# A spectral filter and a token mixer on one core: the first batch's turn, rearranged

## The chip, the core and the metric

The kernel runs on one core of a Trainium2 chip. TensorE (PE) multiplies, VectorE (DVE), ScalarE (ACT) and GpSimd (POOL) work beside it, SyncE (SP) and POOL issue the transfers. The metric is device time in microseconds of one execution; lower is better.

## What is computed

For 8 batches of a 3136 x 256 matrix x: a Fourier filter along the sequence, and on its result u a low-rank mixing of the sequence (rank 32) and an MLP over the channels.

```python
X = np.fft.rfft(x, axis=1)
x = np.fft.irfft(X * (filt_r + 1j * filt_i), n=3136, axis=1)
xt = x.transpose(0, 2, 1)
u = x + (xt @ U @ V).transpose(0, 2, 1)
out = u + np.maximum(u @ w_ch1, 0.0) @ w_ch2      # 256 -> 1024 -> 256
```

## The kernel before

3136 is 64 x 49, and the transform is done in two steps: a 64-point one (F1, constant `w64`) and a 49-point one for each of 32 frequencies s, with the twiddles in it (`t2` forward, `g12` back). Between the two steps the layout changes from sequence rows to frequency rows. For batches 1 to 7 that goes through DRAM: F1 (`f1_units`, 13 units of a batch, each one matmul of 512 columns and a copy to `asb`; after the units 2, 5, 8 and 12 a chunk is stored to `c1`), then `load_a` of eight frequencies at a time, then a *pair* (two frequencies): `forward` to px, the product with the filter on VectorE, and two pairs later the inverse (`i1`) to esb, stored to `c2` every four pairs; `load_e` brings it back as e2. From e2, `h1_unit` makes H1 = U's spectrum times e2, and `make_u` makes u for four rows at a time: a low-rank matmul with V (`vr`) and H1, and four with e2 and the inverse transform `s2`, in one PSUM bank for each half of the channels, copied to `ut`. A *group* of four rows then goes through `mm1` (eight hidden tiles, relu) and `mm2` (with u added through an identity matrix).

Batch 0 has no other batch to hide behind, and goes without DRAM: `first_f1`, `first_a` and `first_mid` transpose on PE instead. `first_mid` runs 16 pairs m; DVE's product of each (128 x 1024) is the densest work there. In the spare time of PE and ACT lie the first units of batch 1 (`next(fill)`), dummy matmuls `keep_on`, and U's spectrum `prep_u` (two PSUM banks, copied by ACT to `usb`). After the last pair, the transposes L389 make e2 in seven pieces (k4), copied by DVE and ACT in turn, and `h1_unit(0)` and `make_u(0)` follow.

V has to come in the order of the rows, on 128 partitions: `v_order` (POOL, L241) reorders it in seven pieces `vp` of 32 partitions, and `v_units` (L248) spreads each with a matmul by `sel` (four identity matrices) and copies it on ACT to `vr`. Piece k serves group k of every batch.

The order of the work is written by hand: each engine does its instructions in the order of the program, and waits follow from data and buffers. The main loop (L670) gives each group eight *slots*; after every two mm1 tiles and after every mm2 row `run(slot)` issues what `put` has placed there: units, pairs (`steps`, L639), loads, V's pieces, H1. Group 0 has no mm2 beside it, so slots 0 to 7 are short. On SP's queue stand the stores of batch 1's chunks, all `load_a`, `load_e` and the stores to `c2`, in the order of the slots; on POOL's the loads of x and, before the main loop, V's reordering between the loads of batch 2's first chunks (L628).

PSUM has eight banks: four "m" (mm1, units, V, u, transposes, batch 0's px), two "o" (mm2, U, batch 0's transposes, early units), one "x" (a pair's px), one "f" (inverse, H1). A bank is written again when its copy is done.

Of the kernel before, what the change touches and what calls it, by code (L numbers as in the profile page):

```python
# [9 lines left out]
F16 = mybir.dt.float16  # L10
# [7 lines left out]
RANK = 32  # L18
ESC = 16.0
NH = 25  # L20
# [5 lines left out]
def _consts():  # L26
    n, half = SEQ, SEQ // 2
    r = np.arange(NR)
    q = np.arange(NQ)


    w = np.zeros((NQ, NS, 2))
    for s in range(NS):
        w[:, s, 0] = np.cos(2 * np.pi * s * q / NQ)
        w[:, s, 1] = -np.sin(2 * np.pi * s * q / NQ)
    w[:, 0, 1] = (-1.0) ** q
    w = w.reshape(NQ, 64)
    w64 = np.zeros((128, 128))
    w64[:64, :64] = w
    w64[64:, 64:] = w  # L40
    s2 = np.zeros((128, 128))
    s2[:64, :64] = w.T / ESC
    s2[64:, 64:] = w.T / ESC


    t2 = np.zeros((NS, 98, 128))
    g = np.zeros((NS, 128, 98))
    for s in range(NS):
        for j in range(49):
            if j < 25:  # L50
                f = s + 64 * j
                e, sg = np.exp(-2j * np.pi * f * r / n), 1.0
            elif s:
                f = 64 * (j - 24) - s
                e, sg = np.exp(-2j * np.pi * (n - f) * r / n), -1.0
            else:
                f = 32 + 64 * (j - 25)
                e, sg = np.exp(-2j * np.pi * f * r / n), 1.0
            ei = np.conj(e)
            if s:  # L60
                t2[s, :49, j], t2[s, 49:, j] = e.real, -e.imag
                t2[s, :49, 64 + j], t2[s, 49:, 64 + j] = sg * e.imag, sg * e.real
                g[s, j] = np.concatenate([ei.real, ei.imag]) * 2
                g[s, 64 + j] = np.concatenate([-ei.imag, ei.real]) * 2 * sg
            else:
                o = 0 if j < 25 else 49
                t2[s, o:o + 49, j] = e.real
                t2[s, o:o + 49, 64 + j] = e.imag
                g[s, j, o:o + 49] = ei.real * (2 if f else 1)
                g[s, 64 + j, o:o + 49] = -ei.imag * 2  # L70

    t2[0, :, 64] = 0
    t2[0, 49:, 64] = (-1.0) ** r
    g[0, 64] = 0
    g[0, 64, 49:] = (-1.0) ** r
    g *= ESC / n
    gs = np.concatenate([g[:, 64:], g[:, :64]], 1)
    f16 = np.float16
    return (w64.astype(f16), s2.astype(f16), np.eye(128).astype(f16),
            np.tile(np.eye(32), (1, 4)).astype(f16),  # L80
            np.ascontiguousarray(t2.transpose(1, 0, 2).reshape(98, NS * 128)).astype(f16),
            np.ascontiguousarray(np.stack([g, gs], 1).transpose(2, 0, 1, 3)
                                 .reshape(128, NS * 2 * 98)).astype(f16))
# [3 lines left out]
def kernel(  # L87
# [30 lines left out]
    def bank(tag, name):  # L118
        return ps.tile([128, 512], F32, tag=tag, bufs=BUFS[tag], name=name)
# [78 lines left out]
    load_rest()  # L198
    for c in range(2, len(CH)):
        load_x(0, c)  # L200
    sel = cst.tile([32, 128], F16)
    nc.sync.dma_start(sel, sel_d.ap())
    s2 = cst.tile([128, 128], F16)
    nc.sync.dma_start(s2, s2_d.ap())
# [24 lines left out]
    usb = cst.tile([128, NH * RANK], F16)  # L229
    nc.vector.memset(usb[64:128, (NH - 1) * RANK:NH * RANK], 0.0)  # L230

    vps = []

    def v_order():

        for r0 in range(0, NH, 4):
            n, nh = (4, 2) if r0 < NH - 1 else (1, 1)
            vp = sb.tile([32, 512], F16, tag="h", bufs=18, name="vp")
            dst = vp[:, 0:n * nh * 64].rearrange("p (r h q) -> p r h q", h=nh, q=64)
            for k, v in enumerate(vqs):  # L240
                nc.gpsimd.tensor_copy(  # L241
                    dst[:, :, :, 32 * k:32 * k + 32],
                    bass.AP(tensor=v.tensor, offset=v.offset + r0,
                            ap=[v.ap[0], [1, n], [NH, nh], [NR, 32]]))
            vps.append((r0, n * nh * 64, vp))
            yield

    def v_units():  # L248

        for r0, n, vp in vps:  # L250
            pv = bank("m", "pv")
            nc.tensor.matmul(pv[:, 0:n], sel[:, :], vp[:, 0:n], start=True, stop=True)
            nc.scalar.copy(vr[:, r0 * 128:r0 * 128 + n], pv[:, 0:n])
            yield

    def new_e2(b):
# [2 lines left out]
        st[b]["e2"] = e2  # L259
        return e2  # L260

    def prep_u():
        for n0, nn in ((0, 16), (16, 9)):
            pu = bank("o", "pu")
            for h in range(2):
                m = (min(nn, NH - h - n0)) * RANK
                a = (h * NH + n0) * RANK
                nc.tensor.matmul(pu[64 * h:64 * h + 64, 0:m], w64[0:64, 0:64], uq[:, a:a + m],
                                 start=True, stop=True)
            m = (min(nn, NH - 1 - n0)) * RANK  # L270
            nc.scalar.copy(usb[:, n0 * RANK:n0 * RANK + m], pu[:, 0:m])
            if m < nn * RANK:
                nc.scalar.copy(usb[0:64, n0 * RANK + m:(n0 + nn) * RANK],
                                      pu[0:64, m:nn * RANK])


    at = sb.tile([128, 2 * 64 * NR], F16, tag="e2", bufs=2, name="at")
# [53 lines left out]
    def first_mid(fill):  # L331
# [26 lines left out]
        for m in range(NS // 2):  # L358
            for k, part in enumerate(PARTS):
                if k and 2 * m == part[0]:  # L360
                    swap_real(*part)
                    swap_imag(*part)
            uv = both_products(m, pxs.pop(0))
            if pend is not None:
                back(*pend)
            pend = (m, uv)
            if m + 2 < NS // 2:
                pxs.append(ahead(m + 2))
            if m + 3 < NS // 2:
                first_a(m + 3)  # L370
            if m in (3, 7, 11):
                keep_on(12)
            if m > 12:
                keep_on(12, "m")
            if m in (9, 10, 11, 14, 15):
                next(fill)
            if m == 14:
                prep_u()
        back(*pend)
        keep_on(8, "m")  # L380
        e2 = new_e2(0)
        for k4, n0 in enumerate(range(0, NH, 4)):
            pt = ps.tile([128, 1024], F16, tag="m", bufs=BUFS["m"], name="pe")
            w = min(4, NH - n0)
            k = 64 if w == 1 else 128
            for rr in range(w):
                for dh in range(2):
                    o, a = rr * DM + dh * 128, (dh * NH + n0 + rr) * 128
                    nc.tensor.transpose(pt[0:k, o:o + 128], et[:, a:a + k], idn[:, :])  # L389
            dst = e2[0:k, n0 * DM:(n0 + w) * DM]  # L390
            (nc.scalar.copy if k4 in (1, 4, 6) else nc.vector.tensor_copy)(dst, pt[0:k, 0:w * DM])
            if k4 == 3:
                next(fill)
            if k4 == 5:
                next(vgen)

    def f1_units(b, both):
        ne = 0
        for c in range(len(CH)):
            xt = st[b]["x"].pop(c)  # L400
            asb = sb.tile([128, 7 * DM], F16, tag="asb", bufs=3, name="asb")
            for n0 in range(0, CH[c], 2):
                w = min(2, CH[c] - n0) * DM
                k = 64 if c0[c] + n0 == NH - 1 else 128
                pf = bank("o" if b == 1 and ne < 6 else "m", "pf")
                nc.tensor.matmul(pf[0:k, 0:w], w64[0:k, 0:k], xt[0:k, n0 * DM:n0 * DM + w],  # L406
                                 start=True, stop=True)
                dst = asb[0:k, n0 * DM:n0 * DM + w]
# [115 lines left out]

    def u_part(b, r0, nr, half, pm, o, dh):

        e2, h1 = st[b]["e2"], st[b]["h1"]
        k = 64 if half else 128
        nc.tensor.matmul(pm[:, o:o + nr * k], h1[:, dh * 128:(dh + 1) * 128],  # L529
                         vr[:, r0 * 128:r0 * 128 + nr * k], start=True, stop=False,  # L530
                         skip_group_check=True)
        for rr in range(nr):
            a = (r0 + rr) * DM + dh * 128
            nc.tensor.matmul(pm[:, o + rr * k:o + (rr + 1) * k], e2[0:k, a:a + 128],  # L534
                             s2[0:k, 0:k], start=False, stop=(rr == nr - 1),
                             skip_group_check=True)

    def make_odd(b):
# [10 lines left out]
    def make_u(gx):  # L549
        b, r0, nr = groups[gx]  # L550
        if nr == 1:
            make_odd(b)
            uts[gx] = odd[b // 2]
            return
        uts[gx] = sb.tile([128, 1024], F16, tag="ut", bufs=3, name="ut")
        for dh in range(2):
            pm = bank("m", "pu")
            u_part(b, r0, nr, False, pm, 0, dh)
            nc.scalar.copy(uts[gx][:, dh * 512:(dh + 1) * 512], pm)  # L559

    def mm1(gx, t):
        w = groups[gx][2] * 128
# [71 lines left out]
    vgen = v_units()  # L634
    first_mid(fill)
    next(h1_unit(0))
    make_u(0)

    steps = [10 + 1.4 * k for k in range(NP)] + [33 + 2.87 * k for k in range(NP)]  # L639
    for k in range(7):  # L640
        put(k // 2, fill)
    for b in range(3, nb):
        steps += [SB * (b - 2) + 31 + 3 * k for k in range(NP)]
    steps += [steps[-1] + 3 * (k + 1) for k in range(LAG)]
# [6 lines left out]
    for b in range(1, nb):  # L651
        for gi in range(NS // KG):
            t = steps[NP * (b - 1) + GP * gi]
            put(t - (5 if b == 1 else 8), one(load_a, b, gi))
        put(SB * b - 4, h1_unit(b))
        if b > 1:
            fill = f1_units(b, b == 2)
# [5 lines left out]
                if b > 2:  # L663
                    put(steps[NP * (b - 1)] - 68 + 10 * c, one(load_x, b, c))

    for k in range((NH - 1) // 4):
        put(1 + 2 * k, vgen)

    slot = 0
    for gx in range(len(groups) + 1):  # L670
# [47 lines left out]
```

## Time and profile before

| | us |
|---|---|
| median of 3 executions | 561.04 |
| lowest, highest | 560.57, 564.15 |
| the profiled execution: time, span | 561.33, 559.6 |
| PE busy in the span | 532.6 (95%) |
| ACT, DVE, POOL busy | 363.3, 367.3, 248.8 |
| PE idle before its px at 66.05, waiting for a load | 1.91 |
| DVE idle before its first e2 copy at 44.69 | 3.19 |
| mean of one pair product of batch 1 on DVE (L448) | 1.219 |
| copies of 128 x 512 from PSUM: ACT L559, DVE L597 | 0.598, 0.692 |

Busy time counts a matmul with its way through the array, so several in a row overlap. The chain of work that ended last is followed back from the end, from each piece to what released it. PEclk is the share of full speed that PE's clock was granted.

### The profile page before, as it was taken

What the parts mean: (1) busy time and instruction counts of PE and PEld (TensorE: products, weight loads), DVE (VectorE), ACT (ScalarE), POOL (GpSimd) and SP (SyncE); (2) the same over time, 40 slices, a digit from 0 to 9 for tenths busy, and PEclk for the clock granted to TensorE, in tenths of its full rate; (3) what the DMA queues carried; (4) which work ended last, traced back from release to release, by engine and by line L of the source; (5) the groups of instructions that cost most, each with busy time, mean ns of one, the idle gap of its engine ahead of it and who ended that gap; (6) DMA issues with size and microseconds to landing.
All of it is one profiled execution on the core that took longest, in us unless ns stands there. A gap on an engine that the chain in (4) does not pass through costs nothing.

```text
span 559.6 us, 11747 instructions
## 1 busy us (share of the span) xinstructions
PE 532.6 (95%) x4530; PEld 381.4 (68%) x4530; DVE 367.3 (66%) x531; ACT 363.3 (65%) x731; POOL 248.8 (44%) x356
## 2 busy tenths in 40 slices
PE   4788899999999999999999999999999999999996
PEld 4675477767677767677776767777677767767665
DVE  7993376657777577767777577767777587424342
ACT  3777666767767586777767586677666576654441
POOL 7678031255556455555556365555444344210000
PEclk9899899999999999999999999999999999999999
DMA  8999669767979857787879757786757544631223
GB/s 139 209 207 227 196 152 224 152 172 172 205 178 212 190 135 164 169 195 184 205 167 204 171 134 166 180 209 166 178 156 156 139 111 96 139 86 42 74 77 84
DMA packets 67897, 89.83 MB, mean 161 GB/s; under 512 B 6881, under 2 KB 53506, under 8 KB 66946
## 3 DMA queue, kind: packets, MB, share of 16 engines
q0 software_dynamic: 19120, 50.37, 40.8%
q1 hardware_dynamic: 48642, 38.65, 28.9%
q8 instruction: 35, 0.57, 0.5%
q14 instruction: 20, 0.16, 0.1%
q10 hardware_dynamic: 80, 0.07, 0.0%
HBM read 56.80 MB, written 48.17 MB: 188 GB/s over the span
## 4 chain that ended last, share of the span: by engine, by line
PE 82%; DVE 4%; DMA 3%; ACT 2%; issue 1%; SPq 0%; ACTq 0%; DVEq 0%
PE po L588 30%; PE phh L566 28%; PE pi L476 4%; PE px L440 4%; PE po L592 4%; PE pu L529 4%; PE pu L534 4%; PE pf L406 3%; DVE uv L461 1%; ACT h L573 1%; DMA e<-c 1%; PE ph L507 1%; DMA c<-esb 1%; DVE uv L459 1%; DMA a<-c 1%
## 5 line engine op out<-in xcount | busy, mean ns | idle before, releaser
L573 ACT ACTIVATE h<-phh 128x512 f16<-128x512 f32 (+1 forms) x350 | 186.6, 575 | 107.0 <-PE phh L566 106.6
L588 PE MATMUL po<-w,h 128*128 128x256 f16 x1568 | 204.0, 273 | 0.0
L566 PE MATMUL phh<-ut,w 128*128 128x512 f16 x768 | 197.7, 379 | 0.6 <-ACT ut L559 0.2
L464 POOL TENSOR_TENSOR y<-uv 128x512 f16<-128x512 f16 x96 | 110.3, 1149 | 150.2 <-DVE uv L461 71.0
L588 PEld LDWEIGHTS <-h 128*128 128x128 f16 x1568 | 150.4, 98 | 36.4
L461 DVE TENSOR_TENSOR uv<-px,ft 64x512 f16<-64x512 f32 x192 | 132.1, 688 | 2.6
L597 DVE COPY och<-po 128x512 f32<-128x512 f32 x96 | 66.4, 692 | 81.8 <-PE po L592 80.4
L566 PEld LDWEIGHTS <-w 128*128 128x128 f16 x832 | 74.7, 98 | 53.1 <-issue 3.5
L459 DVE TENSOR_TENSOR uv<-px,ft 128x512 f16<-128x512 f32 x96 | 66.0, 688 | 56.0 <-PE px L440 54.0
L480 ACT CAST esb<-pi 98x512 f16<-98x512 f32 x112 | 65.8, 588 | 39.7 <-PE pi L476 32.0
L605 POOL DMA_DIRECT2D out_dram<-och x84 | 45.6, 547 | 60.9 <-DVE och L597 60.9
L412 ACT CAST asb<-pf 128x512 f16<-128x512 f32 (+1 forms) x82 | 46.6, 570 | 16.4 <-PE pf L406 16.4
L440 PE MATMUL px<-a,t 98*128 98x256 f16 x256 | 49.6, 276 | 6.6 <-DMA a<-c 2.8
L559 ACT CAST ut<-pu 128x512 f16<-128x512 f32 x96 | 51.8, 598 | 2.2 <-PE pu L534 1.9
L592 PE MATMUL po<-idn,ut 128*128 128x128 f16 x384 | 52.9, 219 | 0.0
L571 DVE TENSOR_SCALAR h<-phh 128x512 f16<-128x512 f32 (+1 forms) x66 | 42.9, 649 | 13.9 <-PE phh L566 13.4
L448 DVE TENSOR_TENSOR uv<-px,ft 128x1024 f16<-128x1024 f32 x32 | 38.0, 1219 | 10.1 <-PE px L440 9.7
L534 PEld LDWEIGHTS <-e 128*128 128x128 f16 (+1 forms) x400 | 30.9, 97 | 17.7 <-issue 2.5
L416 POOL DMA_DIRECT2D c<-asb x48 | 26.0, 548 | 33.9 <-ACT asb L412 26.5
L529 PE MATMUL pu<-vr,h 128*128 128x512 f16 (+1 forms) x112 | 39.6, 354 | 1.4 <-ACT h L511 0.5
L592 PEld LDWEIGHTS <-ut 128*128 128x128 f16 x384 | 37.7, 98 | 4.4
L534 PE MATMUL pu<-s,e 128*128 128x128 f16 (+1 forms) x400 | 40.3, 218 | 0.0
(72 smaller groups left out, 378.5 us busy)
## 6 DMA issues: line engine op xcount, KB each, us to landing
out_dram<-och POOLq DMA_DIRECT2D x84, 256.0 KB, 4.3
a<-c SPq DMA_DIRECT2D x28, 392.0 KB
c<-esb SPq DMA_DIRECT2D x28, 392.0 KB
xt<-in_x_dram POOLq DMA_DIRECT2D x56, 192.0 KB, 5.8
c<-asb POOLq DMA_DIRECT2D x42, 192.0 KB, 3.3
e<-c SPq DMA_DIRECT2D x28, 200.0 KB, 4.4
e<-c SPq DMA_DIRECT2D x28, 192.0 KB, 5.6
out_dram<-och SPq DMA_DIRECT2D x12, 256.0 KB, 3.3
```

The lines of the kernel that those rows point to most:

```text
L440: nc.tensor.matmul(px[:, sl * DM:(sl + 1) * DM], t2[:, s * 128:(s + 1) * 128], a2[:, (2 * ml + sl) * DM:(2 * ml + sl + 1) * DM], start=Tru ...
L459: nc.vector.tensor_mul(uv[:, 0:512], px[:, :], ft[:, a:a + 512])
L461: nc.vector.tensor_mul(uv[p:p + 64, 512:1024], px[q:q + 64, :], ft[q:q + 64, b:b + 512])
L464: nc.gpsimd.tensor_add(y, uv[:, 0:512], uv[:, 512:1024])
L480: nc.scalar.copy(esb[:, ml * 512:(ml + 1) * 512], pi[0:98, :])
L529: nc.tensor.matmul(pm[:, o:o + nr * k], h1[:, dh * 128:(dh + 1) * 128], vr[:, r0 * 128:r0 * 128 + nr * k], start=True, stop=False, skip_gr ...
L534: nc.tensor.matmul(pm[:, o + rr * k:o + (rr + 1) * k], e2[0:k, a:a + 128], s2[0:k, 0:k], start=False, stop=(rr == nr - 1), skip_group_chec ...
L566: nc.tensor.matmul(pm[:, 0:w], w1[:, dh * 1024 + t * 128:dh * 1024 + (t + 1) * 128], ut[:, dh * w:(dh + 1) * w], start=(dh == 0), stop=(dh ...
L573: nc.scalar.activation(h[:, 0:w], pm[:, 0:w], RELU)
L588: nc.tensor.matmul(po[:, o:o + DM], hs[gx, t][:, rr * 128:(rr + 1) * 128], w2[:, t * DM:(t + 1) * DM], start=(t == 0), stop=False, skip_gr ...
L592: nc.tensor.matmul(po[:, o + dh * 128:o + (dh + 1) * 128], ut[:, dh * w + rr * 128:dh * w + (rr + 1) * 128], idn[:, :], start=False, stop= ...
L597: nc.vector.tensor_copy(och[:, a:(rr + 1) * DM], po[:, 0:(rr + 1) * DM - a])
```

## The change

In `first_mid`, batch 1's units come at m = 8, 9, 10, 13, 14, 15 (before: 9, 10, 11, 14, 15 and k4 = 3), the sixth in an "m" bank; the dummy matmuls of m = 15 go. U's matmuls stay at m = 14, both parts in a row; their copies move behind the last pair and from ACT to DVE.

`make_u(0)` becomes `first_u`: the four spectrum matmuls of both halves first, then V's pieces 1 and 2 (before in slots 1 and 3), then the low-rank matmul of each half and its copy, the first on ACT, the second on DVE. V's pieces 0, 1, 2 are copied by DVE, the others by ACT; pieces 3 to 6 come in slots 6, 8, 10, 12 (before 5, 7, 9, 11). Those four have 128 rows: POOL first clears the whole tile (a memset ahead of each reordering), and `sel` has zeros in 96 more rows.

In the main loop, the seven units left come in slots 0, 1, 1, 2, 2, 3, 3 (before 0, 0, 1, 1, 2, 2, 3); batch 1's pairs in slots from 12 on, 1.3 apart (before from 10, 1.4 apart); batch 1's loads six slots before their first pair instead of five, those of the other batches nine instead of eight. The pairs of batch 2 and all that follows keep their slots.

```diff
+    vps = [(r0, 512 if r0 < NH - 1 else 64,
+            sb.tile([128, 512], F16, tag="h", bufs=18, name="vp")) for r0 in range(0, NH, 4)]
     def v_order():
-        for r0 in range(0, NH, 4):
+        for r0, w, vp in vps:
...
-            vp = sb.tile([32, 512], F16, tag="h", bufs=18, name="vp")
-            dst = vp[:, 0:n * nh * 64].rearrange("p (r h q) -> p r h q", h=nh, q=64)
+            if r0 > 8:
+                nc.gpsimd.memset(vp[:, 0:w], 0.0)
+            dst = vp[0:32, 0:n * nh * 64].rearrange("p (r h q) -> p r h q", h=nh, q=64)
...
     def v_units():
...
-            nc.tensor.matmul(pv[:, 0:n], sel[:, :], vp[:, 0:n], start=True, stop=True)
-            nc.scalar.copy(vr[:, r0 * 128:r0 * 128 + n], pv[:, 0:n])
+            k = 128 if r0 > 8 else 32
+            nc.tensor.matmul(pv[:, 0:n], sel[0:k, :], vp[0:k, 0:n], start=True, stop=True)
+            (nc.scalar.copy if r0 > 8 else nc.vector.tensor_copy)(vr[:, r0 * 128:r0 * 128 + n], pv[:, 0:n])
...
-            if m > 12:
+            if m in (13, 14):
                 keep_on(12, "m")
-            if m in (9, 10, 11, 14, 15):
+            if m in (8, 9, 10, 13, 14, 15):
                 next(fill)
             if m == 14:
-                prep_u()
+                pus = [prep_u(0, 16), prep_u(16, 9)]
+                for pu in pus:
+                    next(pu)
         back(*pend)
         keep_on(8, "m")
         e2 = new_e2(0)
+        for pu in pus:
+            next(pu, None)
...
-            if k4 == 3:
-                next(fill)
...
-                pf = bank("o" if b == 1 and ne < 6 else "m", "pf")
+                pf = bank("o" if b == 1 and ne < 5 else "m", "pf")
...
+    def first_u():
+        pms = [bank("m", "pu") for dh in range(2)]
+        for dh in range(2):
+            u_spec(0, 0, 4, False, pms[dh], 0, dh, True)
+        next(vgen)
+        next(vgen)
+        uts[0] = sb.tile([128, 1024], F16, tag="ut", bufs=3, name="ut")
+        for dh in range(2):
+            u_rank(0, 0, 4, False, pms[dh], 0, dh, False)
+            (nc.vector.tensor_copy if dh else nc.scalar.copy)(
+                uts[0][:, dh * 512:(dh + 1) * 512], pms[dh])
...
-    make_u(0)
-    steps = [10 + 1.4 * k for k in range(NP)] + [33 + 2.87 * k for k in range(NP)]
+    first_u()
+    steps = [12 + 1.3 * k for k in range(NP)] + [33 + 2.87 * k for k in range(NP)]
     for k in range(7):
-        put(k // 2, fill)
+        put((k + 1) // 2, fill)
...
-            put(t - (5 if b == 1 else 8), one(load_a, b, gi))
+            put(t - (6 if b == 1 else 9), one(load_a, b, gi))
...
-    for k in range((NH - 1) // 4):
-        put(1 + 2 * k, vgen)
+    for k in range(3, 7):
+        put(2 * k, vgen)
```

`u_spec` is the four matmuls of `u_part` with e2 and `s2`, `u_rank` the one with H1 and `vr`; `prep_u(n0, nn)` is one part of the old `prep_u`, with a `yield` between its matmuls and its copies.

## The prediction

> **What bounds the kernel now.** I read the page's 40 slices first, then a table of 1 us stretches, the chain that ended last, and the time lines of PE, ACT and DVE from 36 to 75 us.
>
> ```profile
> PE   4788899999999999999999999999999999999996
> PEclk9899899999999999999999999999999999999999
> DMA  8999669767979857787879757786757544631223
> ```
>
> From slice 6 on (70 us), PE is busy without a break up to the tail: whatever the change does to the end, it does before about 122 us (slot 44, batch 1's H1), by letting PE reach the same point sooner. The change touches 30 to 104 us. In it the one low clock digit is slice 5. The stretches show why (columns: PE, PEld, DVE, ACT, POOL busy, then granted clock, DMA share, GB/s):
>
> ```profile
> 64.00:65.00 1.00, 0.14 (x1) 0.00 (x0) 0.00 (x0) 0.83 (x2) 0.19 (x1) 1.00 1.08 308
> 65.00:66.00 1.00, 0.00 (x0) 0.00 (x0) 0.00 (x0) 0.00 (x0) 0.00 (x0) 1.00 0.99 234
> 66.00:67.00 1.00, 0.95 (x6) 0.69 (x6) 0.53 (x1) 0.27 (x1) 0.00 (x0) 0.77 0.91 272
> 67.00:68.00 1.00, 1.00 (x7) 0.69 (x5) 0.69 (x1) 0.31 (x1) 0.00 (x0) 0.50 0.83 266
> 68.00:69.00 1.00, 1.00 (x7) 0.58 (x5) 0.42 (x1) 0.00 (x0) 0.00 (x0) 0.50 1.11 273
> 69.00:70.00 1.00, 1.00 (x4) 0.33 (x4) 1.00 (x2) 0.21 (x1) 0.00 (x0) 0.52 0.42 130
> ```
>
> PE stands still from 64.14 to 66.05, and then the clock is halved for 3.4 us. The chain names the waits of the whole start:
>
> ```profile
> 46.25 0.59 ACT asb L412
> 46.83 0.91 ACT e L391
> 47.74 0.49 ACT vr L253
> 48.23 0.26 ACT e L391
> ...
> 49.93 1.08 ACT ut L559 x2
> ...
> 52.33 0.70 DVE asb L410
> ...
> 55.51 0.70 DVE asb L410
> ...
> 62.43 3.58 DMA a<-c
> ...
> 70.41 0.61 DVE asb L410
> ```
>
> Three kinds: ACT copies in front of H1 and the first ut (46 to 51), PSUM banks of slots 0 to 3 that wait for a copy (two gaps of PE, about 0.77 each), and batch 1's first load (pair 0, slot 10), whose wait and clock are the dearest: 1.91 + (0.23 + 0.50 + 0.50 + 0.48 = 1.71) = 3.6 us.
>
> **The change, part by part**, on the profiled execution's time, 561.33 us (span 559.6, and 1.7 around it); it stands 0.29 above the median of the three runs, 561.04.
>
> *Units moved into batch 0's pairs (m = 8, 13, k4 = 3).* Unit 3 now comes at m = 13, at 39.2 on PE. Its input, x(1,1), was issued at 31.12 and 31.65 and took 7.8 and 8.1 to land: 39.75. So PE waits 0.6; before, PE came at 40.21. Unit 0 at m = 8 comes at 31.3, its input was there at 30.8: nothing. Then from rows: back 0.36, keep 0.67, unit 4, U's first spectrum, and the second one, which still waits for unit 4's copy on ACT (0.34 before, 0.5 now), back, unit 5 (0.22), back; the keep of m = 15 (0.67) falls away, and so do U's copies on ACT (0.87 + 0.18). By this walk the transposes start at 44.35 instead of 44.03, +0.3. Bounds: -0.3 if x(1,1) is in time, +0.6 if it lands 0.3 later. The units' stores go with them: chunk 0's pair on SP one pair earlier, chunk 1's at about 44 instead of 46.86; SP's queue holds nothing else until the next store, so nothing waits behind them.
>
> *U's copies on DVE.* DVE idles 3.19 us before its first e2 copy at 44.69; the copies (0.69, 0.4, 0.2 by rows of these sizes) fit in. Without that cover they would cost 1.3. Usb's reader comes at 47.6.
>
> *e2's copies.* ACT loses unit 5's copy (0.48 start to start) and V's first (0.49), PE one matmul (0.22). H1's last matmul ends 4.45 after the transposes' start, 4.79 before: -0.3. With the line above, H1 comes at the same time.
>
> *First u.* Eight spectrum matmuls (0.44) go into H1's copy on ACT (0.39). But V's units 1 and 2 come before u's low-rank part on PE, and their copies before ut's second half on DVE, in order. From H1's end: spectra 0.44, V 0.4 to its result, then three DVE copies 0.60 apart and 0.69 for the last: 0.44 + 0.4 + 0.6 + 0.6 + 0.69 = 2.74 to ut, against 2.18 (48.82 to 51.00). +0.5. The first mm1 pair ends late by this; in return two V matmuls (0.3 each) and two ACT copies (0.54 each) leave slots 1 and 3. The 128 rows cost nothing by rows: V's matmul with 32 rows takes 0.38, a unit's with 128 rows and the same 512 columns 0.38. The larger selector is loaded at 2.09 on SP and read at 47: nothing.
>
> *Slots 0 to 11.* Slots 0 to 9 hold 9.7 us of PE work by start-to-start rows (12 mm1 5.2, 11 units 2.3, V 0.4, u 0.9, one mm2 1.0), and V's two matmuls less than before; 51.06 to 64.0 is 12.95 now. ACT is the dense engine there (9.66 of 11 us); it loses V's copies and slot 0 one unit. Walking the four banks by copy rows (ACT 0.54, DVE 0.60 a piece) gives 1.3 us of gaps instead of 2.2 to 2.6, so slot 10 is reached 11.1 us after the start, at 62.6, and slot 12 at 65.1. If both 0.77 gaps return, 66.0.
>
> *Pair 0 at slot 12.* Unit 12's copy ends at 55.9 (56.42 before), and from there to the load's landing the old chain took 9.6 us (store 56.4 to 62.2, load 62.43 to 66.05): 65.5. POOL's queue: the memsets in front of V's last units have only the 64x256 one as a row, 0.31 us; three of 128x512 cost 0.9 (each like that row) to 1.9 (twice the columns, twice the time). I take 1.5. They move x(2,1) by 0.5 and x(2,2), x(2,3) by 1.5, off the path (needed from slot 9, 61 us; landed by 59 to 62), but into the store's way: store and load between 64.9 and 67.9. I take 65.5 to 66.05, as DMA was full until 59.5 in either order. PE is then at most 1 us early, and I count no halved clock.
>
> *The sum.* At 71.06 PE began group 2's u. In the new order pair 0 (65.75), unit (0.22), V's last (0.11) put it at 66.1; the 0.44 of pairs 0 and 1 that were done then are still owed: 66.5, a gain of 4.5.
>
> *Pairs at 1.3 slots.* A pair at slot 8j+3 or 8j+7 has an och copy ahead of it on DVE; if the next slot has a pair too, PE waits about 0.55 (twice now: 89.06 to 91.13 and 95.33 to 97.41, 2.07 against 1.52 of work). New slots are 12, 13, 15, 16, 17, 19 to 22, 24 to 26, 28 to 30, 32: two such neighbours again, one softened by a unit, and four of 0.19: 1.6 against 1.25. +0.3.
>
> *Loads for batches 2 on, one slot sooner.* SP works in order and its stores wait for ACT. For batches 3 to 7 a load lands in the slot of a store and still behind it: nothing. For batch 2, two loads move ahead of a store; their readers come nine slots later: nothing, for they are no piece of the chain there.
>
> Sum: -4.5 + 0.3 = -4.2; if gaps return, about -3.7. I take -4.0: 557.3 beside 561.33, 557.1 on the scale of the median.
>
> **A rule against the trace.** The row: 1.91 us without work, then 3.4 us at half clock. The Trainium skill, "TensorE: Matmul & The Clock Gate", Part 1, has the clock drop after an idle window of about 3.4 us and tells one to avoid gaps over some 3 us. By that rule a stall of 1.9 us would not have done it, the cause would remain, and the 1.71 would not come back: 558.8. The trace speaks against it: the drop begins 0.4 us after the stall.
>
> **The rivals.**
> *Clock not won.* A half-clock stretch comes anyway, from the gaps at 49 to 53 or of 39 to 43, where a keep is taken out (18.8 to 22.2 is one that nothing here touches). It costs up to 3.4 x 0.5 = 1.7: 558.8. For it: PE will be idle some 1.3 us before ut. Against it: the stretch 49 to 53 now has as much idle and kept 1.00.
> *The wait moves along.* The x loads, later by the memsets, hold up the last store; pair 0 starts at 67.9, PE has waited 2.8 us, and the clock halves: 66.1 + 2.2 + 1.7 = 70.0 where 66.5 stood: gain 0.5, 560.5. For it: DMA is at 1.0 to 1.1 until 59. Against: store bytes and last issue are earlier.
> *DVE bound by the pairs.* With fewer PE pieces between pairs, and DVE copies of batch 2's units in slots 12 to 18, each neighbour could cost 0.55. It undoes the gain from 7 to 8 such waits beyond today's two; with all 15 pairs, 13 x 0.55 = 7.2, and the kernel is slower: 561.1 - 4.2 + 7.2 = 564. Against it: DVE has 9 to 11 us of work in 12 to 14 of a group.
> *Everything fits.* x(1,1) in time (-0.6), no gap at pair 0 (-0.6), gaps of slots 0 to 3 gone: 555.5.
>
> **How the numbers follow.** Forecast 0.50 (own range 555.8 to 558.3); clock not won 0.13; the wait moves along 0.15; DVE bound 0.10; everything fits 0.12. From 555.0, under the best case, to 561.8, over the case of the moved wait, leaves out most of DVE bound and the worst of the best case's tail, together under 2 in 10. One per cent, about what a measurement of this kernel tells from no change, is 5.6 us: faster means under 555.4, which half of "everything fits" and a tail of the forecast reach: 0.12. Slower means over 566.6: the far end of DVE bound, 0.05. The rest, 0.83, is within 1%.
>
> **What would show it.** Right: no idle over 1 us before pair 0's px, near 65.5; clock 1.00 from 60 to 72; H1 copied near 48.8; the first ut's second half on DVE near 51.5, two V copies just ahead of it; PE waits at L406 of unit 3 near 39.2. Wrong: a long "DMA a<-c" still in the chain; a clock of 0.5 in 40 to 72; ACT still before H1; many pieces "DVE uv" between 66 and 100, or POOL late with V's units 1 and 2.

## The result, and the profile after

The changed kernel takes 565.08 us (median of 20 executions, 559.89 to 570.05), the kernel before 560.67 (20, 558.18 to 564.15): the ratio is 1.0064, with a 95% interval of 1.0041 to 1.0088. It is taken over the fast runs alone (19 with a mean of 564.44, 20 with 560.84), so it is not the quotient of the medians. The change costs 3.6 us where the forecast had 4.0 won. The profiled execution of after took 566.45 us, with a span of 564.7.

The two rows of the page of after that answer to those of before:

```profile
PE   5788799989999999999999999999999999999996
PEclk9989989999999999999999999999999999999999
```

The low clock digit of slice 5 is now in slice 6 (70.6 to 84.7 us), and there is one in slice 3, of which more below. The stretches show the same picture as before, 5 us later: PE still, then half the clock (columns as above).

```profile
69.00:70.00 1.00, 0.00 (x0) 0.00 (x0) 0.24 (x1) 0.09 (x1) 0.83 (x2) 1.00 1.07 226
70.00:71.00 1.00, 0.43 (x3) 0.29 (x3) 0.02 (x1) 0.00 (x0) 1.00 (x3) 1.00 1.18 248
71.00:72.00 1.00, 1.00 (x8) 0.61 (x7) 1.00 (x1) 0.80 (x3) 0.28 (x1) 0.66 1.07 212
72.00:73.00 1.00, 1.00 (x8) 0.87 (x7) 0.21 (x1) 0.73 (x2) 0.00 (x0) 0.50 1.24 276
73.00:74.00 1.00, 1.00 (x7) 0.69 (x6) 0.00 (x0) 0.26 (x1) 0.00 (x0) 0.50 1.08 336
```

And the chain that ended last, between 60 and 130 us, has four transfers more than "DMA a<-c" at 62.43:

```profile
66.38 4.14 DMA a<-c
...
85.50 6.66 DMA c<-esb
...
93.05 6.23 DMA a<-c
...
113.02 5.78 DMA c<-esb
...
119.18 5.90 DMA e<-c
...
125.32 1.09 PE ph L511 x25
```

These are three waits of PE: at pair 0 (2.17 us), at pair 12, slot 28 (0.45), and at batch 1's H1, slot 44 (2.56). Before, pair 12 did not wait, and H1 waited 0.67 for ACT and for no transfer.

From point to point in the two profiled executions (before, after; the difference of the spans is 5.1):

| stretch | before | after | difference |
|---|---|---|---|
| to the last product of batch 0 | 41.26 | 42.37 | +1.1 |
| to H1's copy on ACT | 7.58 | 8.09 | +0.5 |
| to the second mm1 matmul | 2.22 | 2.81 | +0.6 |
| to group 2's u, with 0.44 owed for pairs 0 and 1 | 20.0 | 18.2 | -1.8 |
| to H1 of batch 1, less the 0.44 | 49.6 | 53.9 | +4.3 |
| to the end | 438.9 | 439.4 | +0.4 |

The first row differs from execution to execution: in the profiles below, the last product ends between 40.8 and 43.9 where unit 0 comes at m = 8, and between 41.3 and 43.8 where it comes at m = 9. But after has a wait in it that before has not. Unit 0 of batch 1, in the profiled executions before and after:

```profile
32.65 0.38 PE L406 MATMUL pf<-xt,w 128*128 128x512 f16 x1
```

```profile
33.19 0.39 PE L410 MATMUL pf<-xt,w 128*128 128x512 f16 x1 [2.04 <-DMA xt<-in_x_dram]
```

At m = 8 PE waits there for the load of x(1,0), and here the clock is halved from 33.8 to 37.2 (the low digit in slice 3). With unit 0 at m = 8 seven of twelve profiles have such a wait (0.23 to 2.04 us), with unit 0 at m = 9 none of six.

The fifth row holds the half clock after pair 0, which came ahead of group 2's u before and comes behind it now (1.7), and the waits at H1 (1.9 more) and pair 12. In the last, another half-clock stretch, 125.9 to 129.3, follows H1's wait.

### The profile page after: what moved, and what is told of

It reads as the page before. It is cut to its first block, busy times and chain, and to the rows that moved or that the text cites. A ratio compares the mean times of both kernels' runs of the same rounds, so it can differ in the third digit from the quotient of the medians.

```text
span 564.7 us, 11727 instructions
## 1 busy us (share of the span) xinstructions
PE 534.1 (95%) x4518; PEld 382.0 (68%) x4518; DVE 371.3 (66%) x538; ACT 360.6 (64%) x724; POOL 250.7 (44%) x360
## 4 chain that ended last, share of the span: by engine, by line
PE 78%; DMA 7%; DVE 3%; ACT 1%; issue 1%; SPq 0%; ACTq 0%; DVEq 0%
PE po L614 29%; PE phh L592 26%; PE pi L480 4%; PE px L444 4%; PE po L618 4%; PE pu L537 4%; DMA a<-c 4%; PE pu L547 4%; PE pf L410 2%; DMA c<-esb 2%; DVE uv L465 1%; PE ph L511 1%; DMA e<-c 1%; ACT h L599 1%; DVE uv L463 1%
## 5 line engine op out<-in xcount | busy, mean ns | idle before, releaser
L444 PE MATMUL px<-a,t 98*128 98x256 f16 x256 | 49.6, 275 | 6.3 <-DMA a<-c 3.0
```

The costliest lines, as they stand in the source:

```text
L444: nc.tensor.matmul(px[:, sl * DM:(sl + 1) * DM], t2[:, s * 128:(s + 1) * 128], a2[:, (2 * ml + sl) * DM:(2 * ml + sl + 1) * DM], start=Tru ...
```

## The experiments

Below, x(b,c) is the load of chunk c of x for batch b, load (b,g) is the `load_a` number g of batch b (c and g count from 0), and e is what `load_e` brings for H1. Three theories came out of these lines. S: the memsets hold POOL's x loads back, these the last store of batch 1's chunks, and pair 0 waits. P: the pairs' new slots put the first store to c2 (slot 19 instead of 17) into the time of the load of x(3,1), and SP holds load_e and load (1,3) behind it. L: load (2,1), one slot sooner, passes batch 1's last store to c2 on SP, and H1 waits. Against them stood E, that the early part is the loss, and N, that one execution misled.

**The changed kernel again** (a0), no edit.

> The changed kernel once more, beside the kernel before on the same chip, for a second profile. Theory S (the store): the x loads that stand behind the memsets on POOL hold up batch 1's last store, so pair 0 waits about 2 us for its load near 70 and the clock halves after it; it will be seen again, and the ratio stays near 1.006. Theory E (early part): the transposes start about 1 us late counted from the last product of batch 0, and the first mm1 pair another 0.6 late; seen again too. Theory N (chance): the 1.1 us by which the last product was late in the first profile, and the long waits after slot 20, are not seen again, and the ratio is under 1.004.

1.0068 (1.0043 to 1.0093). Pair 0 waits 2.81, half clock from 70.4; pair 12 waits 2.14, half clock from 101.2; H1 waits 1.00. N is out. The transposes start 3.4 us after the last product (3.8 in the first profile, 2.8 before); PE waits 0.70 for x(1,1) at unit 3.

**No memsets, 32 rows** (a1; once more as d3).

```diff
-            if r0 > 8:
-                nc.gpsimd.memset(vp[:, 0:w], 0.0)
-            k = 128 if r0 > 8 else 32
+            k = 32
```

> The changed kernel without the four memsets: all of V's pieces are spread with 32 rows as before. Theory S: the loads of x(2,2) and x(2,3) are issued about 2 us sooner (near 53 instead of 55.3), the last store lands sooner, pair 0 waits under 1 us, and the time falls by 2 to 3.5 us, to a ratio of 1.000 to 1.002. Theory E: the memsets are beside the point, the ratio stays at 1.005 to 1.007. If the 128 rows themselves keep the clock up, a half-clock stretch appears between 55 and 66 that the changed kernel does not have.

1.0024 (0.9995 to 1.0053); its second run, d3 below, 1.0024 too. Pair 0 does not wait, and no clock is halved between 40 and 130 us: the 128 rows are not needed for a full clock. POOL's time line before its last x loads, of after and then without memsets:

```profile
50.68 0.55 POOL L240 MEMSET vp<- 128x512 f16 x1
51.29 1.41 POOL L243 COPY vp<-vq 32x256 f16<-32x256 f16 x2
52.66 0.51 POOL L240 MEMSET vp<- 128x512 f16 x1
53.23 1.40 POOL L243 COPY vp<-vq 32x256 f16<-32x256 f16 x2
54.58 0.14 POOL L240 MEMSET vp<- 128x64 f16 x1
54.78 0.41 POOL L243 COPY vp<-vq 32x32 f16<-32x32 f16 x2
55.27 2.06 POOL L136 DMA_DIRECT2D xt<-in_x_dram  x4
```

```profile
48.54 3.15 POOL L241 COPY vp<-vq 32x256 f16<-32x256 f16 x6
51.64 2.06 POOL L136 DMA_DIRECT2D xt<-in_x_dram  x4
```

From V's first reordering (42.56, 41.04) that is 12.7 against 10.6 us. A memset of 512 columns takes 0.51 to 0.55.

**Batch 0's pairs as before** (a2), **and the first u as before** (a4), each undone in the changed kernel.

> The changed kernel with batch 0's pairs as before: units at m = 9, 10, 11, 14, 15 and k4 = 3, the dummies of m = 15 kept, U's copies on ACT right behind its matmuls. Theory E: from the last product to the first transpose 2.8 us as before instead of 3.8, but ACT's copies come back in front of H1 (about 0.5): a gain of 0.5 to 1.0 us, ratio 1.005. Theory S: pair 0 waits as long as in the changed kernel, as its load sets the time: no gain, 1.006.

1.0034 (1.0006 to 1.0063). The last product to the transposes is 2.77 again, to H1's copy 7.29 (8.09 in after). Pair 0 waits 1.49, H1 2.27. These points are as E has them, but the interval reaches both theories.

> The changed kernel with the old first u: low-rank part first, V's pieces 1 to 6 in slots 1, 3, 5, 7, 9, 11, all of V copied by ACT, ut by ACT. Theory E: H1's end to the second mm1 matmul is 2.2 us again instead of 2.8, but two matmuls of V and two ACT copies return to slots 1 and 3 (about 1 us): ratio 1.006 to 1.008. Theory S: slot 12 is reached later, pair 0's load not: no difference, as the wait is only shorter: 1.006.

1.0027 (0.9996 to 1.0059), less than either theory had, with an interval that reaches both. Pair 0 waits 1.59, pair 12 1.91, H1 2.03: the waits of S, P and L are all there without the new first u. In a2 and in a4 the clock stays whole after pair 0, where after and a0 lose 1.7 us, 0.003 of the time; so much of what these two runs win may be that.

**Loads eight slots ahead again**, without memsets (b1) and in the changed kernel alone (d4).

```diff
-            put(t - (6 if b == 1 else 9), one(load_a, b, gi))
+            put(t - (6 if b == 1 else 8), one(load_a, b, gi))
```

> No memsets, and the loads of batches 2 on eight slots ahead again instead of nine. Theory L (the loads): load (2,1), one slot sooner, passes batch 1's last store to c2 on SP and takes the transfers ahead of it; with eight the order on SP is the old one, the store lands in 4 to 4.5 us instead of 5.1 to 5.8, and H1 of batch 1 does not wait for e any more (1.0 to 2.6 us in the four profiles): 1.5 to 2 us less than with nine. Theory P (the pairs' slots): the loads are beside the point, H1 still waits 1 to 2.5 us, and pair 12 waits 0.3 to 2 us for its load.

0.9983 (0.9954 to 1.0013). SP's time line around batch 1's last store, of before, of after and of this kernel:

```profile
110.21 0.33 SPq L482 DMA_DIRECT2D c<-esb  x1
110.58 0.52 SPq L425 DMA_DIRECT2D a<-c  x1
114.43 0.78 SPq L432 DMA_DIRECT2D e<-c  x2
```

```profile
108.49 0.36 SPq L429 DMA_DIRECT2D a<-c  x1
113.02 0.33 SPq L486 DMA_DIRECT2D c<-esb  x1
118.82 0.78 SPq L436 DMA_DIRECT2D e<-c  x2
```

```profile
111.14 0.33 SPq L484 DMA_DIRECT2D c<-esb  x1
111.51 0.78 SPq L427 DMA_DIRECT2D a<-c  x1
114.58 0.79 SPq L434 DMA_DIRECT2D e<-c  x2
```

SP issues load_e when the store has landed. With the load behind the store that is 4.2 and 3.4 us; with the load 4.5 us ahead of it, 5.8, and e comes too late for slot 44. In all profiles it is 4.5 to 5.8 with the loads nine slots ahead, 3.4 to 4.8 with eight. Here H1 waits 0.67 for ACT, as before, and pair 12 still waits 1.35.

> The changed kernel with one edit: loads of batches 2 on eight slots ahead instead of nine. Theory L: H1 of batch 1 does not wait for e (0.7 us for ACT instead, as before), pair 0 and pair 12 wait as in the changed kernel; 1.5 to 2 us less, ratio 1.002 to 1.004. If L is wrong: 1.006.

1.0021 (0.9996 to 1.0045), against 1.0064 with nine. H1 waits 0.67 for ACT; pair 0 waits 2.56 and pair 12 2.16. In ten profiles with loads nine ahead H1 waited for e in nine (1.0 to 2.6 us); in eight with eight, once (1.14).

**The pairs' slots**: old ones, with the old loads, without memsets (b2), and new ones, with the new loads, as the only part in the kernel before (b3).

> No memsets, and batch 1's pairs and all loads in their old slots (from 10, 1.4 apart; loads 5 and 8 ahead). Theory P: the first store to c2 is issued ahead of the loads of x(3,1) again and lands in 3 to 4 us instead of 6 to 7, neither pair 12 nor H1 waits for a transfer; pair 0 waits about 2 us near 64 to 66 as before, with a halved clock after it. The sum is about that of the kernel before, less V's pieces out of the slots: ratio 0.998 to 1.000. If P is wrong, the waits at pair 12 and H1 stay and the ratio is 1.004 or more.

0.9993 (0.9961 to 1.0026). Pair 0 waits 1.45 (no clock halved), pair 12 and H1 for no transfer.

> The kernel before with one part of the change alone: pairs from slot 12, 1.3 apart, loads 6 and 9 ahead. Theory P with L: pair 0 does not wait (PE reaches slot 12 about when the load lands, 66 to 67), no halved clock there, 3 us won; but pair 12 waits 0.3 to 2 us and H1 of batch 1 for e 1 to 2.5 us, one of them with a halved clock in some executions: ratio 0.995 to 1.000. My prediction on record would have it at 0.993 without these waits.

0.9998 (0.9967 to 1.0030). Pair 0 does not wait, so my 3.6 us are won; pair 12 waits 0.40, H1 waits 2.32 and the clock is halved after it. On average they give it all back.

**Pairs that join the old slots at 17**, without memsets (b4; c1 and c2 undo or mend more of it), and in the kernel before (c4).

```diff
-    steps = [12 + 1.3 * k for k in range(NP)] + [33 + 2.87 * k for k in range(NP)]
+    steps = [max(12 + k, 10 + 1.4 * k) for k in range(NP)] + [33 + 2.87 * k for k in range(NP)]
-            put(t - (6 if b == 1 else 9), one(load_a, b, gi))
+            put(t - (6 if b == 1 else 8), one(load_a, b, gi))
```

> No memsets, loads eight ahead, and pairs from slot 12 that are one slot apart until they meet the old slots at 17 (pair 5). Theory P: pair 0 as without memsets, no wait or one under 0.5 us; the first store to c2 in its old slot 17, so it lands in 3 to 4.5 us and pair 12 does not wait; H1 does not wait for e. The price is five neighbours at 0.2 to 0.55 us, 1.5 us in all: ratio 0.995 to 0.998, and faster than the kernel before.

0.9971 (0.9941 to 1.0001). No wait at pair 0, none for a load at pair 12. SP's time line at the first store to c2, before, in after and here:

```profile
80.92 0.31 SPq L482 DMA_DIRECT2D c<-esb  x1
84.10 0.78 SPq L432 DMA_DIRECT2D e<-c  x2
```

```profile
85.50 0.31 SPq L486 DMA_DIRECT2D c<-esb  x1
92.23 0.78 SPq L436 DMA_DIRECT2D e<-c  x2
93.05 0.41 SPq L429 DMA_DIRECT2D a<-c  x1
```

```profile
82.20 0.31 SPq L484 DMA_DIRECT2D c<-esb  x1
85.35 0.78 SPq L434 DMA_DIRECT2D e<-c  x2
86.17 0.41 SPq L427 DMA_DIRECT2D a<-c  x1
```

The store lands in 3.2 us, as before, instead of 6.7, and load (1,3) goes out 4.0 after the store instead of 7.6. In after, POOL had issued a chunk's store at 84.11 and x(3,1) at 85.16; before, the x load followed the c2 store by 3.6 us. In all twelve profiles with pairs 1.3 apart from slot 12 the store takes 6.6 to 7.1 us to land, and pair 12 waits for its load (0.3 to 2.2 us); in the six with the old or the joined slots the store takes 3.1 to 3.4, and pair 12 does not wait.

> The kernel before with one part alone, mended: pairs from slot 12, one slot apart up to slot 17, then the old slots; loads six and eight ahead. Theories P and L: no wait at pair 0, none at pair 12, none for e at H1; against the kernel before 3.6 us of wait and clock are gone and up to 1.5 us of neighbours come: ratio 0.995 to 0.998. If it is as fast as the joined pairs with the rest of the change (0.997), the rest brings nothing.

0.9960 (0.9937 to 0.9983): 0.4% faster than the kernel before, with these two lines alone (the first slots, and batch 1's loads six ahead). Pair 0 waits 0.27.

> The joined pairs without memsets and with the loads eight ahead, and batch 0's pairs as before (units at 9, 10, 11, 14, 15 and k4 = 3, U's copies on ACT). Theory E: from the last product to H1's copy 7.3 us, as where this was undone alone, instead of 8.1 to 9.3: 0.8 us less than the joined pairs alone, ratio 0.995 to 0.997. If the transposes' delay were hidden behind the load of pair 0, no difference.

0.9958 (0.9934 to 0.9982); pair 0 waits 0.62, H1 1.14 for e. From the last product to H1's copy it is 7.30, as E has it, but the interval overlaps that of the joined pairs alone: E's 0.8 us is not shown in the time.

> The same, and in the first u the low-rank part and ut's two copies ahead of V's pieces 1 and 2. Theory E: H1's copy to the first mm1 that needs the second half falls from 2.8 to about 1.6 us (spectra 0.44, low rank 0.4, one copy 0.69), as the second half no longer stands behind two copies of 0.6 on DVE: 1 us less if the slots are not held up by V's later copies, ratio 0.993 to 0.996. Rival: slots 0 to 3 are bound by the copies of the banks, and pair 0 then waits for its load by as much: no difference.

0.9968 (0.9942 to 0.9994). H1's copy to the first mm1 falls from 2.05 to 1.51 and its second matmul no longer waits, but the time does not fall, as the rival had it. These three are not told apart by their intervals; what c1 and c2 hold beyond c4 (V by DVE, spectra first) adds nothing that shows.

**Memsets on DVE, 128 rows** (c3, again d2); **memsets on POOL, 32 rows** (d1).

> The changed kernel with its four memsets on DVE at the start of the program, beside the one that is there, instead of on POOL among V's pieces: the 128 rows stay. Theory S (the memsets cost as time on POOL's queue): x(2,2) is issued 10.6 us after V's first reordering instead of 12.5 to 12.8, pair 0 waits under 0.5 us, and the ratio is 1.001 to 1.003, as without memsets. If the 128 rows or the larger tiles cost anything themselves, pair 0 waits on and the ratio stays at 1.006.

1.0040 (1.0003 to 1.0077). The x loads go out 10.6 us after V's first reordering, as without memsets, but pair 0 waits 2.70, and the clock is halved from 68.0 on, before the wait ends. S alone does not give this.

> The changed kernel with its memsets on POOL, but V's matmuls read 32 rows only. Theory S (the memsets' time on POOL): x(2,2) is issued 12.5 us after V's first reordering, pair 0 waits 1.5 to 3 us as in the changed kernel, ratio 1.005 to 1.007. Rival R (the 128-row matmuls): pair 0 waits under 1 us, ratio 1.001 to 1.003.

1.0061 (1.0033 to 1.0089), pair 0 waits 2.35: the 128 rows are not needed for the loss.

> The memsets on DVE and 128 rows once more. Theory S: the 2.7 us of pair 0's wait were this execution's (PE came to slot 12 early, 14.2 us after the first mm1 instead of 15.2), the second profile shows under 1.5 us, and the ratio is 1.002 to 1.003. Rival R: a wait of over 2 us again, ratio 1.004 to 1.006.

1.0059 (1.0026 to 1.0093), pair 0 waits 2.70 again.

> No memsets and 32 rows once more. Both theories: pair 0 waits under 1 us, H1 of batch 1 waits 1 to 2.5 us for e and pair 12 0 to 2 us; ratio 1.001 to 1.003.

1.0024 (0.9998 to 1.0051), pair 0 waits 0.85, pair 12 2.19, and H1 only 0.67, for ACT, which neither theory had.

Counted from the last product, pair 0 starts after 25.5 and 25.3 us without memsets, 26.3 and 26.5 with them on DVE, 25.8 to 28.2 on POOL (after, a0, a2, a4, d1, d4). With the memsets on DVE, counted so, it is not the store that lands later. SP issues load (1,0) when the store has landed: 21.2 us after the last product in c3 and d2, 21.5 and 21.3 without memsets, 21.6 to 24.0 with them on POOL. It is the load: from its issue to pair 0 pass 5.0 and 5.3 us in c3 and d2, 4.0 in d3. In four profiles POOL issues its next chunk store 0.8 to 1.1 us ahead of this load (a0, c3, d1, d2), and there it takes 5.0 to 5.3; in the nine others where pair 0 waits it takes 3.6 to 4.6. This goes together in the profiles, but no run changes it alone.

So the memsets on POOL are enough for the loss (d1), but the late store that S speaks of is only a part of it: in d1 load (1,0) goes out only 0.2 to 0.4 later than without memsets. With the memsets on DVE PE also comes to slot 12 sooner (14.2 us after the first mm1 instead of 15.2): two of its gaps behind copies on DVE, 0.78 and 0.31, are missing. That lengthens a wait without costing time. Why c3 and d2 stay at 1.004 and 1.006 is open, with intervals that reach the 1.0024 without memsets.

## Why the prediction was wrong, step by step

*Loads one slot sooner: "nothing".* Wrong. I looked at the loads' readers, nine slots on, and at nobody who queues behind them. One of them passes a store whose landing SP waits for, on the way to H1. Undone alone it moves the ratio from 1.0064 to 1.0021, 2.4 us; the two intervals just touch, and the wait for e is gone.

*Pair 0 at 65.5 to 66.05.* Wrong. The memsets came out within the bounds (1.61 for the three large ones, 1.75 in all), but I kept the store's landing on the old chain's 9.6 us, although the x loads were moved into its way: from the end of its issue to pair 0 it took 11.2 in after (59.39 to 70.57) instead of 8.4 (57.65 to 66.05). The rival "the wait moves along" is what happened, 2.17 instead of 2.8 and with the clock; I gave it 0.15. Without memsets the ratio is lower by 0.0040, 2.2 us, in part by the load and not the store, as said.

*Pairs from 12, 1.3 apart: +0.3.* The term I counted, neighbours on DVE, was small (waits of 0.6 in all, 0.8 before). The one I left out was the pairs' own stores: each pair that moves takes its c2 store along on SP, here into the x load's time, 6.7 us instead of 3.2. Joined slots without memsets, 0.9971, against 0.9983: the intervals overlap; the waits in the profiles are the evidence.

*Units: +0.3, within -0.3 to 0.6.* The wait for x(1,1) was forecast: 0.6. It is there in seven of the twelve profiles with unit 3 at m = 13, 0.27 to 1.16 us. In six of these (all but b4, where the clock is halved as well) the transposes start 2.7 us after the last product plus just this wait; without it they start 2.7 to 2.8 after it (b2, d1, d3), as before. So the units' other pieces added nothing that shows. Wrong was "nothing" for unit 0: x(1,0) was not in time at m = 8 in seven of twelve. In after PE waits 2.04 there, with half a clock behind it, and the transposes start 3.8 after the last product with no wait for x(1,1); so they do in b1 (3.6), after a half clock from 27 to 34.

*E2's copies, first u, V's matmuls, U's copies on DVE.* Right: the transposes to H1's copy 4.30 against 4.81; from H1's copy to the second mm1 2.81 against 2.22, +0.6 for +0.5; 32 and 128 rows both 0.38; U's copies ran in DVE's idle time.

*Slots 0 to 11 and the clock.* By the table, -1.8 to group 2's u with pair 0's wait in it. The forecast had PE at slot 12 13.6 us after mm1's start (51.5 to 65.1); from the second mm1 matmul to there it takes 15.1 in after, 13.4 to 14.6 in the other eleven profiles with this first u and pair 0 at slot 12. With no wait at pair 0 the clock stayed whole there (a1, b1, b3, b4), and where pair 0 waited 1.9 us or more it was halved in five of seven profiles. The rule that I weighed from the Trainium skill, "TensorE: Matmul & The Clock Gate", Part 1, tells of gaps over some 3.4 us. The runs disagree: those five gaps were of 1.9 to 2.8 us. After gaps of 2.70 (d2) and 2.56 (d4) the clock stayed whole all the same. The half-clock stretches here last 3.3 to 3.4 us, or twice that (6.8 us, before 35 us, in b1 to b4 and c2). The Trainium skill, same page and part, has a window of 3.4 us that runs freely. That would fit both, but no run here tests it.

The sum was therefore short of the transfers that three of its parts hold up. Two steps add up on their own: 1.0064 - 0.0040 - 0.0043 = 0.9981, and both undone together gave 0.9983; with intervals of 0.003 to either side that can be luck, and the old first u (-0.0037) and batch 0's old pairs (-0.0030) won nearly as much when undone alone. With all three undone the ratio is 0.9971 (b4), where the forecast, 557.1 beside 561.04, was 0.9930. Which term holds these last 2.3 us no run shows.

## What to carry to other kernels

When an instruction is moved, ask for its queue: which transfer does it now pass, and who waits for that one's landing; a reader nine slots away says nothing about it. A load or a store that starts later is not free: here it came into the way of, or behind, another on the critical path (6.7 us to land instead of 3.2). A part that wins its wait can lose it at the next wait of the same loop, so each part should be tried alone: of this change, one edit, the pairs' first slots and their loads with the old slots kept from 17 on, brought 0.4% by itself.

## What the runs showed of the hardware

The same transfer of 392 KB to DRAM, batch 1's first store to c2, landed in 3.1 to 3.4 us in six profiles and in 6.6 to 7.1 in twelve. In the six POOL issued a chunk's store 2.3 us and an x load 3.6 us behind it, in the twelve 1.4 and 0.3 us ahead of it. A wait of PE is not priced by its length alone: 1.91 us at pair 0 halved the clock for 3.4 us in one execution, 2.70 did not in another, 1.45 and 1.49 not either.
